# Reversed rows of W by DMA, natural channel order, unread matmuls, and split LN sums in a spectral layer with an MLP

## The chip, the cores and the metric

The kernel runs on one core of one Trainium2 chip. A core has five engines with a queue each: TensorE (PE; its weight loads are listed apart as PEld), VectorE (DVE), ScalarE (ACT), GpSimd (POOL) and SyncE (SP), which here only issues DMAs. The metric is device time in microseconds (us). Before the change three runs took 202.03, 202.07 and 204.34 us; the median is 202.07.

## The reference

Two layers on x of 2048 rows by 512 channels, bf16 in and out:

```
h   = x + spectral(layernorm(x))          # layernorm without gain, eps 1e-5
h2  = h + mlp(layernorm(h))
spectral(u) = irfft2(rfft2(u, axes rows and channels) * (w_r + 1j*w_i))   # w: 2048 x 257
mlp(v)      = relu(v @ w1 + b1)**2 @ w2 + b2                              # w1: 512 x 1792
```

## The kernel before

Rows and channels are transformed by matmuls with tables of sines and cosines that the kernel makes at the start: POOL writes index patterns, DVE or POOL multiplies them, ACT takes the sine. Row index = 16 p + g: partition p of 128, row tile g of 16, so x lies in SBUF as xs[p, g, channel].

*First stage.* For each g the kernel takes LN statistics (`ln1_stats`, lines 182–188: two DVE steps, then POOL's inverse deviation by a power), normalizes (`ln1_norm`, 190–200: DVE, or ACT for the five g in `ON_ACT`), multiplies by the tables KF on PE (`stage1`, 202–212) and ACT casts the PSUM result into Bt. It goes in chunks of x of 2, 2, 4, 4, 4 tiles, which arrive in five DMAs.

*Spectral stage.* Row frequencies k and 16 − k are handled together: pairs pr = 0 to 7 (pair 0 holds frequencies 0 and 8). `stage2` (318–327) transforms channels (table GF), ACT casts into U; `stage3` (329–352) transforms rows (table EF), ACT casts into AB; `spectral` (354–385) on DVE forms sums and differences X (the butterfly), multiplies by W (mA, mB), combines them into Z and then M; POOL does channels 0 and 256, which are real (`real_channels`); `stage4` (387–408) goes back along rows (table EI) and ACT casts into T2. Even and odd channels lie apart (e j order), in X, W and M.

*W.* Wn holds W as loaded, 16 rows a partition. POOL scales the rows 0 to 8 into WB (`w_direct`, 216–225). The rows 9 to 15 are needed with the partitions reversed: `w_reversed` (276–293) multiplies by the mirror matrix J on PE, and DVE and ACT scale the result into WB. `w_real` (295–303) makes the coefficients SD of the two real channels.

*MLP stage.* For each row tile g, `s5` (450–461) goes back along channels (table GI; DVE makes R from two halves), `s6` (463–469) finishes the rows, adds x and takes LN statistics; `rstd` (471–475) on POOL makes the inverse deviation and hb = h + b2; `norm` (480–491), `transp` (493–508). Then `up` (537–544: four matmuls, Relu on ACT, square on DVE) over 14 blocks of 128 hidden channels and `down` (548–558). Chunks are of 2, 2, 4, 4, 4 tiles (`CHUNKS`), and `run` (567–578) puts the preparation of the next chunk, step by step, between the MLP's slots of this one, in equal numbers to a slot.

Each engine takes its instructions in the order of the program: `pin` (22–31) fixes that order. Tiles of PSUM come from a pool of four buffers (first two stages) and of 3 + 3 + 2 banks (MLP stage). All loads and stores are issued on SP, in the order x, W, w1, w2, b1, b2 (lines 97–105).

Of the kernel before, what the change touches and what calls it, by code (L numbers as in the profile page):

```python
# [9 lines left out]
ALU = mybir.AluOpType  # L10
# [5 lines left out]
P = 128  # L16
# [18 lines left out]
def kernel(  # L35
# [28 lines left out]
    wrv = A_w_r.rearrange("(k j) l -> k j l", j=16)  # L64
    wiv = A_w_i.rearrange("(k j) l -> k j l", j=16)
# [9 lines left out]
    mhalf = persist.tile([P, 4], FP32, name="mhalf")  # L75
    KI = persist.tile([P, P], BF16, name="KI")
    GI = persist.tile([P, 4, 256], BF16, name="GI")
    T2 = persist.tile([P, 4, G, 16, 8], BF16, name="T2")
# [3 lines left out]
    J = fwd.tile([P, P], BF16, name="J")  # L82
    vs = fwd.tile([P, 2, 7, 2], FP32, name="vs")
    WB = [fwd.tile([P, 8, 2, 256], BF16, name=f"WB{i}") for i in range(2)]
# [15 lines left out]
    for i, wv in enumerate((wrv, wiv)):  # L100
        nc.sync.dma_start(Wn[i][:], wv)
# [12 lines left out]
    def sin_of(dst, fi):  # L114
# [18 lines left out]

    nc.gpsimd.iota(pI[:, 0:1], pattern=[[0, 1]], base=0, channel_multiplier=1)
# [5 lines left out]
    nc.gpsimd.iota(subc[:], pattern=[[0, 16], [1, 8]], base=0, channel_multiplier=0)  # L140
    nc.gpsimd.iota(idxL[:].rearrange("p (r e j) -> p r e j", r=2, e=2), pattern=[[0, 2], [1, 2], [2, 128]], base=0,
                   channel_multiplier=0)
    nc.gpsimd.memset(idxL[:, 256:257], 256)
    nc.gpsimd.memset(mhalf[:], -0.5)
    nc.gpsimd.iota(idxK[:].rearrange("p (a b) -> p a b", a=9), pattern=[[1, 9], [16, P]], base=0, channel_multiplier=0)
# [4 lines left out]
    nc.vector.scalar_tensor_tensor(fiK[:], rowA[:].rearrange("p q s -> p (q s)"), pF[:, 1:2],  # L150
                                   offA[:].rearrange("p q s -> p (q s)"), ALU.mult, ALU.add)

    nc.vector.tensor_scalar(cols[:, 0:1], pF[:, 0:1], 128.0, None, ALU.mult)
    nc.vector.tensor_scalar(cols[:, 1:2], pF[:, 0:1], 128.0, 16384.0, ALU.mult, ALU.add)

# [5 lines left out]
    nc.vector.tensor_scalar(mask[:], subc[:].rearrange("p q s -> p (q s)"), pF[:, 2:3], None, ALU.is_equal)  # L161
    for t in range(2):
        o = 512 * t
        nc.vector.tensor_scalar(fiG[:, o:o + 257], idxL[:, 0:257], cols[:, t:t + 1], float(QT), ALU.mult, ALU.add)
        nc.vector.tensor_scalar(fiG[:, o + 257:o + 512], idxL[:, 257:512], cols[:, t:t + 1], float(HT),
                                ALU.mult, ALU.add)
# [454 lines left out]
```

## Time and profile before

| | |
|---|---|
| median of the runs | 202.07 us |
| the profiled execution | 202.05 us, its span 200.3 us |
| mean granted TensorE clock | 0.939 |
| busy share PE / weight loads / DVE / ACT / POOL | 79 / 44 / 70 / 49 / 28% |
| chain that ended last, shares | PE 58%, DVE 30%, ACT 6%, POOL 3% |
| DMA | 10.27 MB in 7613 packets |

A row of a view of groups gives line, engine, operation, written tile <- read tiles, shape and count, then busy us and mean ns of one, then the idle time just before and what ended it. A row of the order of time begins with start and length in us; in brackets stands how long the engine had been idle and who released it. A row of stretches has the stretch, its length, then busy us and count of PE, weight loads, DVE, ACT and POOL, the granted clock, the DMA share and GB/s. Instructions on one engine overlap at their ends, so the distance of two starts is less than a length.

### The profile page before, as it was taken

To read this page: it belongs to the slowest core of one execution; us is meant where nothing else is said; L and a number is where in the kernel's file an instruction comes from. 1 tells how busy PE (TensorE), PEld (TensorE's weight loads), DVE (VectorE), ACT (ScalarE), POOL (GpSimd) and SP (SyncE) were. 2 spreads that over 40 slices of the span, in tenths; PEclk is the share of its full clock that TensorE was granted. 3 is DMA by queue.
4 is the path that set the end of the run, shared out by engine and by line. 5 is a ranking of instruction groups with operands and counts; after the bars stand their busy time and mean duration, and the time that the engine had idled before them with its cause. 6 is when DMAs were issued, how large, how long until landed. Compare 5 with 4: busy or idle time off the path is not lost.

```text
span 200.3 us, 2641 instructions
## 1 busy us (share of the span) xinstructions
PE 157.7 (79%) x919; PEld 88.8 (44%) x919; DVE 140.2 (70%) x320; ACT 98.5 (49%) x144; POOL 56.2 (28%) x113
## 2 busy tenths in 40 slices
PE   0046959499774450999997699999999999999992
PEld 0024846266452220774773245444554445544440
DVE  7999834958999476498699847886668878344221
ACT  3634788458886111574572357731367703488000
POOL 8558571332252006006000900008200038000000
PEclk9999999958999655699999999999999999999999
DMA  5999910000000000000100000001000000100001
GB/s 167 362 414 391 241 26 3 2 0 0 3 0 2 0 0 0 0 3 2 52 0 3 26 26 0 0 3 52 26 26 3 3 23 29 52 0 3 26 26 52
DMA packets 7613, 10.27 MB, mean 51 GB/s; under 512 B 2224, under 2 KB 6192, under 8 KB 7344
## 3 DMA queue, kind: packets, MB, share of 16 engines
q1 hardware_dynamic: 7600, 10.11, 14.8%
q8 instruction: 7, 0.11, 0.2%
q14 instruction: 6, 0.05, 0.1%
HBM read 8.01 MB, written 2.10 MB: 50 GB/s over the span
## 4 chain that ended last, share of the span: by engine, by line
PE 58%; DVE 30%; ACT 6%; POOL 3%; issue 2%; DVEq 0%; POOLq 0%; ACTq 0%
PE ph L540 22%; PE po L553 22%; DVE st L185 4%; PE p L455 4%; DVE st L468 2%; DVE mA L369 2%; ACT Bt L212 2%; DVE u L490 2%; DVE mB L369 2%; DVE hs L466 2%; PE p L502 2%; PE p L324 1%; DVE Z L371 1%; PE p L209 1%; DVE act L544 1%
## 5 line engine op out<-in xcount | busy, mean ns | idle before, releaser
L540 PE MATMUL ph<-UT,W 128*128 128x512 bf16 (+1 forms) x280 | 54.5, 341 | 0.9 <-DVE UT L508 0.5
L543 ACT ACTIVATE rl<-ph,b1f 128x512 bf16<-128x512 f32 (+1 forms) x70 | 41.5, 602 | 23.0 <-PE ph L540 20.1
L553 PE MATMUL po<-W,act 128*128 128x512 bf16 x224 | 50.8, 379 | 0.4 <-DVE act L544 0.4
L540 PEld LDWEIGHTS <-W 128*128 128x128 bf16 x280 | 27.8, 99 | 23.0 <-issue 2.7
L544 DVE TENSOR_TENSOR act<-rl 128x512 bf16<-128x512 bf16 (+1 forms) x70 | 24.8, 365 | 16.6 <-ACT rl L543 15.8
L553 PEld LDWEIGHTS <-act 128*128 128x128 bf16 x224 | 21.5, 98 | 25.0 <-DVE act L544 0.9
L472 POOL TENSOR_SCALAR rs<-mv 128x4 f32<-128x4 f32 (+1 forms) x5 | 1.3, 260 | 77.9 <-DVE mv L469 77.9
L209 PE MATMUL p<-KF,un 128*128 128x256 bf16 x32 | 10.3, 343 | 15.8 <-DVE un L199 14.7
L557 DVE TENSOR_TENSOR ot<-po,hb 128x512 bf16<-128x512 f32 x16 | 11.0, 689 | 15.1 <-PE po L553 15.1
L487 ACT ACTIVATE u<-hs,nm,rs 128x512 bf16<-128x512 bf16 x8 | 6.2, 808 | 27.3 <-DVE nm L484 27.3
L475 POOL TENSOR_TENSOR hb<-hs,b2b 128x512 f32<-128x512 bf16 x16 | 18.2, 1167 | 0.0
L400 PE MATMUL p<-EI,M 128*128 128x256 bf16 x28 | 8.2, 314 | 6.1 <-DVE M L382 6.1
L502 PE MATMUL p<-ident,u 128*128 128x128 bf16 x64 | 5.7, 231 | 8.0 <-DVE u L490 8.0
L455 PE MATMUL p<-GI,T 128*128 128x256 bf16 x64 | 10.7, 299 | 1.4 <-DVE T L406 1.4
L209 PEld LDWEIGHTS <-un 128*128 128x128 bf16 x32 | 3.8, 119 | 17.9 <-DVE un L199 15.6
L212 ACT CAST Bt<-p 128x1024 bf16<-128x1024 f32 x8 | 7.9, 1014 | 7.8 <-PE p L210 7.8
L468 DVE BATCH_NORM_STATS2 st<-hs 128x6 f32<-128x512 bf16 x16 | 11.1, 695 | 0.6
L466 DVE TENSOR_TENSOR hs<-p,xs 128x512 bf16<-128x512 f32 x16 | 10.9, 681 | 0.0
L408 ACT CAST T<-p 128x1024 bf16<-128x1024 f32 x7 | 7.1, 1014 | 7.6 <-PE p L401 3.9
L185 DVE BATCH_NORM_STATS2 st<-xs 128x6 f32<-128x512 bf16 x16 | 10.7, 668 | 0.0
L210 PE MATMUL p<-KF,un 128*128 128x256 bf16 x32 | 10.4, 346 | 0.0
L490 DVE TENSOR_SCALAR u<-hs,mv,rs 128x512 bf16<-128x512 bf16 x8 | 10.1, 1289 | 0.0
(137 smaller groups left out, 234.0 us busy)
## 6 DMA issues: line engine op xcount, KB each, us to landing
W<-in_B_w_dram SPq DMA_DIRECT2D x2, 1792.0 KB, 18.2
out_dram<-ot SPq DMA_DIRECT2D x16, 128.0 KB, 1.8
xs<-in_A_x_dram SPq DMA_DIRECT2D x3, 512.0 KB, 6.2
Wn<-in_A_w_r_dram SPq DMA_DIRECT2D x1, 1028.0 KB, 10.0
Wn<-in_A_w_i_dram SPq DMA_DIRECT2D x1, 1028.0 KB, 12.0
xs<-in_A_x_dram SPq DMA_DIRECT2D x2, 256.0 KB, 3.8
b2b<-in_B_b_dram SPq DMA_DIRECT2D x1, 128.0 KB, 8.4
b1b<-in_B_b_dram SPq DMA_DIRECT2D x1, 3.5 KB, 21.0
```

The costliest lines, as they stand in the source:

```text
L185: nc.vector.bn_stats(st[:], xs[:, g, :])
L209: nc.tensor.matmul(o, lhsT=un[:, g, P * t:P * t + P], rhs=KFlo, start=True, stop=False)
L212: nc.scalar.copy(dst, pt[:].rearrange("p (e i q s) -> p e i q s", e=4, i=2, q=16))
L455: nc.tensor.matmul(pe[:, 256 * e:256 * e + 256], lhsT=T2[:, lt, g].rearrange("p q s -> p (q s)"), rhs=GI[:, lt, :], start=(r == 0), stop=( ...
L466: nc.vector.tensor_tensor(hs[:, g, :], py[:], xs[:, g, :], ALU.add)
L468: nc.vector.bn_stats(st[:], hs[:, g, :])
L475: nc.gpsimd.tensor_tensor(hb[:, g, :], hs[:, g, :], b2b[:], ALU.add)
L490: nc.vector.tensor_scalar(u2[:, g - a, :], hs[:, g, :], mv2[:, g, 0:1], rs2[:, g:g + 1], ALU.subtract, ALU.mult)
L540: nc.tensor.matmul(ph[:, 0:n], lhsT=W1[:, d, bass.ts(f, P)], rhs=UT[:, d, 0:n], start=(d == 0), stop=(d == ND - 1))
L543: nc.scalar.activation(rl[:, 0:n], ph[:, 0:n], ACT.Relu, bias=b1f[:, f:f + 1], scale=1.0)
L544: nc.vector.tensor_tensor(act[:, f, 0:n], rl[:, 0:n], rl[:, 0:n], ALU.mult)
L553: nc.tensor.matmul(po[:], lhsT=act[:, f, bass.ts(i, P)], rhs=W2[:, f, :], start=(f == 0), stop=(f == NF - 1))
```

## The change

1. *W.* Wn, J, `w_direct` and `w_reversed` go. Two DMAs copy the rows 9 to 15 with partitions reversed from W to a scratch tile in DRAM; four load the rows 0 to 8 straight into WB; two load the scratch into WB (they wait for the copies). All stand on SP between x and w1. WB has rows of 258, of which 257 are used, unscaled: the factor WSC goes into the step of s6 that adds x.
2. *Channel order.* X, W and M are in natural order; stage 2 writes PSUM with a step of two, and stage 4 takes its weights with a step of two. T2 has the row tile outermost; its last evacuation is split 2 tiles on ACT, 7 on DVE, 7 on ACT.
3. *Unread matmuls.* `warm` issues matmuls of a tile of ones (128 x 512) whose result nobody reads: 12, 4, 4, 3 and 2 before stages 1 of g = 0, 2, 4, 8, 12, and 3, 2, 2 and 11 during the preparation of the first MLP chunk.
4. *LN sums split.* For g = 3, 7, 11, 15 ACT makes both sums (two passes that accumulate; their written result is overwritten) and POOL the variance; all normalizations are on DVE. GF's indices move from DVE to POOL, and the order of the table work changes.
5. *Order in the spectral stage.* Stage 3 and stage 2 stand ahead of stage 4 and one pair further on; the two butterfly steps of the next pair stand between those of this one; POOL's products ahead of its sums.
6. *MLP stage.* Chunks of 2, 3, 4, 4, 3; preparation steps in a new order, weighted by time and ready 2.5 (units of the weights) before the end; hb is added on POOL in `up`, each add held back until a given square; the first normalization is on DVE alone.

```diff
-    Wn = [fwd.tile([P, 16, Df], BF16, name=f"Wn{i}") for i in range(2)]
-    WB = [fwd.tile([P, 8, 2, 256], BF16, name=f"WB{i}") for i in range(2)]
+    WB = [fwd.tile([P, 8, 2, 258], BF16, name=f"WB{i}") for i in range(2)]
+    Wrev = [dram.tile([7, P, Df], BF16, name=f"Wrev{i}") for i in range(2)]
...
-        nc.sync.dma_start(Wn[i][:], wv)
+    for i in range(2):
+        nc.sync.dma_start(Wrev[i][:], wvs[i].rearrange("k j l -> j k l")[9:16, ::-1, :])
+    for i in range(2):
+        nc.sync.dma_start(WB[i][:, 0:8, 0, 0:Df], wvs[i][:, 0:8, :])
+        nc.sync.dma_start(WB[i][:, 0, 1, 0:Df], wvs[i][:, 8, :])
+    for i in range(2):
+        nc.sync.dma_start(WB[i][:, 1:8, 1, 0:Df], Wrev[i][:].rearrange("j p l -> p j l")[:, ::-1, :])
...
+    def ln1_sums(g):
+        nc.scalar.activation(un[:, g, :], xs[:, g, :], ACT.Copy, scale=1.0 / D, accum_out=mv1[:, g, 0:1])
+        nc.scalar.activation(un[:, g, :], xs[:, g, :], ACT.Square, scale=float(D) ** -0.5, accum_out=mv1[:, g, 1:2])
...
+    def ln1_rstd(a, b):
+        for g in range(a, b):
+            if g in ON_ACT:
+                nc.gpsimd.tensor_tensor(nm1[:, g:g + 1], mv1[:, g, 0:1], mv1[:, g, 0:1], ALU.mult)
+                nc.gpsimd.tensor_tensor(mv1[:, g, 1:2], mv1[:, g, 1:2], nm1[:, g:g + 1], ALU.subtract)
...
+    def warm(o, n):
+        for _ in range(n):
+            nc.tensor.matmul(o, lhsT=ones[:, 0:P], rhs=ones[:], start=True, stop=True)
...
+    ln1_rstd(0, 2)
+    ln1_sums(3)
+    sin_of(GF[:].rearrange("p t c -> p (t c)"), fiG[:])
+    ln1_stats(2, 4)
+    ln1_rstd(2, 4)
+    table_e(0)
+    ln1_sums(7)
+    ln1_norm(0, 2)
+    stage1(0, 12)
+    ln1_stats(4, 8)
+    ln1_sums(11)
+    table_e(1)
+    ln1_rstd(4, 8)
...
+    ln1_sums(15)
...
     def stage2(pr):
         pu = mm_tile("p2")
-        puv = pu[:].rearrange("p (q r e j) -> p q r e j", q=2, r=2, e=2)
+        puv = pu[:].rearrange("p (q r j e) -> p q r e j", q=2, r=2, e=2)
...
     def stage4(pr, split=False):
-                nc.tensor.matmul(o, lhsT=M[:, 0, r, c0:c0 + P], rhs=ei[:, P:3 * P], start=True, stop=False)
+                nc.tensor.matmul(o, lhsT=M[:, 0, r, e::2], rhs=ei[:, P:3 * P], start=True, stop=False)
...
         if split:
-            nc.scalar.copy(dst[:, :, :, 0:8], src[:, :, :, 0:8])
-            nc.vector.tensor_copy(dst[:, :, :, 8:16], src[:, :, :, 8:16])
+            nc.scalar.copy(dst[:, 0:2], src[:, 0:2])
+            nc.vector.tensor_copy(dst[:, 2:9], src[:, 2:9])
+            nc.scalar.copy(dst[:, 9:16], src[:, 9:16])
...
     stage2(0)
     stage2(1)
     stage3(0)
-    w_reversed()
-    w_real()
     stage3(1)
     stage2(2)
-    spectral(0)
-    for pr in range(1, 9):
-        stage4(pr - 1, split=(pr == 8))
-        if pr + 1 < 8:
-            stage3(pr + 1)
-        if pr + 2 < 8:
-            stage2(pr + 2)
+    w_real()
+    stage3(2)
+    for pr in range(9):
+        if 0 < pr and pr + 2 < 8:
+            stage3(pr + 2)
+        if pr + 3 < 8:
+            stage2(pr + 3)
+        if pr > 0:
+            stage4(pr - 1, split=(pr == 8))
         if pr < 8:
             spectral(pr)
...
-        nc.vector.tensor_tensor(hs[:, g, :], py[:], xs[:, g, :], ALU.add)
+        nc.vector.scalar_tensor_tensor(hs[:, g, :], py[:], WSC, xs[:, g, :], ALU.mult, ALU.add)
...
-    CHUNKS = ((0, 2), (2, 4), (4, 8), (8, 12), (12, 16))
+    CHUNKS = ((0, 2), (2, 5), (5, 9), (9, 13), (13, 16))
...
-            nc.vector.tensor_tensor(act[:, f, 0:n], rl[:, 0:n], rl[:, 0:n], ALU.mult)
+            sq = nc.vector.tensor_tensor(act[:, f, 0:n], rl[:, 0:n], rl[:, 0:n], ALU.mult)
+            if f % 3 == 1 and f // 3 < b - a:
+                g = a + f // 3
+                add = nc.gpsimd.tensor_tensor(hb[:, g, :], hs[:, g, :], b2b[:], ALU.add)
+                tc.add_manual_dep(add.ins, sq.ins.name,
+                                  mybir.DependencyInfo(mybir.DependencyClass.Sync, mybir.DependencyReason.DATA),
+                                  reason="not before this square")
...
+            want = len(prep) if k == len(slots) - 1 else min(len(prep), int(len(prep) * at / (total - 2.5)))
...
-    norm(0, True)
+    norm(0, False)
+    warm(idle[:], 11)
     transp(0, 0)
```

In `spectral` after the change, in the order of DVE: mA, mB, first butterfly step of the next pair, Z (two steps), second butterfly step of the next pair, M (two steps).

More of the change, by code (lines that the diff above doesn't have):

```diff
@@ L132 @@
     kft = tab.tile([P, P], BF16, name="kft")
+    nc.vector.memset(ones[:], 1.0)
     nc.gpsimd.iota(pI[:, 0:1], pattern=[[0, 1]], base=0, channel_multiplier=1)
@@ L166 @@
                                 ALU.mult, ALU.add)
-    sin_of(kft[:], fiK[:])
-    sin_of(GF[:].rearrange("p t c -> p (t c)"), fiG[:])
-    nc.vector.tensor_tensor(KF[:, 0:P], kft[:], mask[:], ALU.mult)
-    nc.vector.tensor_scalar(KF[:, P:2 * P], KF[:, 0:P], -1.0, None, ALU.mult)
-    for i, off in ((0, 0), (1, QT)):
-        nc.gpsimd.tensor_scalar(fiE[i][:], idxK[:], cols[:, 3:4], float(off), ALU.mult, ALU.add)
-        nc.scalar.activation(
-            EF[:, :, i, :], fiE[i][:].bitcast(I16)[:, ::2].rearrange("p (a b) -> p a b", a=9), ACT.Sin,
-            scale=SIN_SCALE)
+    nc.gpsimd.iota(idxK[:].rearrange("p (a b) -> p a b", a=9), pattern=[[1, 9], [16, P]], base=0, channel_multiplier=0)
```

257 lines of the change are left out of this document (119 added, 138 removed).

## The prediction

> **What bounds the kernel now.** I read the page's clock line first, then busy time by stretches cut at the stage borders, then the order of time on each engine inside the stretches that lose. The time outside the span is 202.05 − 200.3 = 1.75 us; the profiled execution (202.05) is at the median of the runs (202.07), so I sum against it.
>
> The page's span and the granted clock in 40 slices of 5 us, then stretches (length; busy us of PE, weight loads, DVE, ACT, POOL; granted clock):
>
> ```profile
> span 200.3 us, 2641 instructions
> PEclk9999999958999655699999999999999999999999
> 40.00:46.00 6.00, 5.87 (x27) 3.72 (x28) 3.64 (x9) 3.04 (x3) 1.88 (x8) 0.50 0.00 0
> 51.80:55.50 3.70, 2.94 (x21) 1.84 (x20) 3.50 (x9) 2.94 (x4) 1.04 (x5) 1.00 0.02 4
> 66.75:81.00 14.25, 5.87 (x27) 3.15 (x27) 7.73 (x15) 2.73 (x5) 3.45 (x6) 0.50 0.00 0
> 80.96:96.73 15.77, 15.64 (x104) 10.35 (x104) 11.21 (x29) 8.30 (x18) 3.39 (x4) 0.92 0.03 10
> 96.70:117.45 20.75, 16.80 (x123) 10.99 (x121) 17.87 (x41) 10.23 (x21) 5.80 (x6) 1.00 0.04 13
> 117.45:145.00 27.55, 27.55 (x148) 13.78 (x148) 19.84 (x42) 13.20 (x21) 5.78 (x6) 1.00 0.06 20
> 173.00:196.80 23.80, 23.71 (x110) 10.54 (x108) 8.29 (x18) 9.62 (x14) 0.00 (x0) 1.00 0.07 23
> ```
>
> From 117.45 on PE is busy the whole time at full clock: 27.55 us for four row tiles with the preparation of four others, 23.80 for four without. So a row tile's MLP costs 5.95 us, a preparation 27.55/4 − 5.95 = 0.94, and sixteen and fourteen of them 95.2 + 13.2 = 108.4 us. Before does it from 80.96 to 196.8, 115.8 us: only 7.4 us can be won there. Of these 96.70–117.45 loses most: two tiles and four preparations are 15.7 us of PE work in 20.75, with DVE busy 17.87. The rest must come from the first 81 us, of which 20.25 us run at half clock.
>
> **First stage, to the first spectral matmul.** DVE sets it; groups by line (count, busy, mean ns), the first statistics, the first stage 2 matmul:
>
> ```profile
> L185 DVE BATCH_NORM_STATS2 st<-xs 128x6 f32<-128x512 bf16 x16 | 10.7, 668 | 0.0
> L186 DVE BATCH_NORM_AGGREGATE mv<-st 128x2 f32<-128x6 f32 x16 | 2.9, 182 | 0.6
> L199 DVE TENSOR_SCALAR un<-xs,mv,rs 128x512 bf16<-128x512 bf16 x11 | 4.1, 422 | 0.0
> L164 DVE TENSOR_SCALAR fiG<-idxL,cols 128x257 int32<-128x257 int32 x2 | 2.4, 1208 | 0.0
> L196 ACT ACTIVATE un<-xs,nm,rs 128x512 bf16<-128x512 bf16 x5 | 4.0, 814 | 0.9 <-DVE nm L193 0.9
> L173 ACT ACTIVATE EF<-fiE 128x1152 bf16<-128x1152 int16 x2 | 2.2, 1146 | 0.0
> L116 ACT ACT_TABLE_LOAD x1 | 1.3, 1283 | 0.7 <-PEq L605 0.7
> L188 POOL TENSOR_TENSOR rs<-rs,mhalf 128x4 f32<-128x4 f32 (+1 forms) x5 | 4.6, 919 | 0.4
> L172 POOL TENSOR_SCALAR fiE<-idxK,cols 128x1152 int32<-128x1152 int32 x2 | 2.7, 1352 | 0.2
> 0.72 2.28 SPq L99 DMA_DIRECT2D xs<-in_A_x_dram  x5
> 6.91 0.69 DVE L185 BATCH_NORM_STATS2 st<-xs 128x6 f32<-128x512 bf16 x1
> 27.30 1.93 ACT L212 CAST Bt<-p 128x1024 bf16<-128x1024 f32 x2
> 29.29 1.92 PE L324 MATMUL p<-GF,Bt 128*128 128x256 bf16 x16 [1.15 <-ACT Bt L212]
> DMA to landing us min/median/max: 3.0/5.4/7.9
> ```
>
> The change takes from DVE four pairs of statistics (4 × 0.85 = 3.4) and the G table's indices (two of 1.21 and two short ones, about 2.8 in sequence); five normalizations come back (5 × 0.42 = 2.1), a fill of ones is new (about 0.2, like other small ones). DVE is relieved by 3.9 us and begins LN at 6.91 − 2.8 + 0.2 = 4.3; it may, because the first chunk of x, issued at 0.72, lands after 3.0 us, at 3.7, and the last, issued by 2.6 (the five issues take 2.28 us), after 7.9, at 10.5. POOL takes the indices where it otherwise waits.
>
> ACT gets eight passes of about 0.81 instead of five, and there they stand in a chain. The second chunk lands at about 5.7 (its landing is the next above 3.0); the sums of tile 3 are done at 7.4, then POOL makes the inverse deviation (0.92 for the power and about 0.7 for the three short steps before it, an estimate from the 0.18 and 0.2 of small ones) and the table's indices (1.35), so the sine starts at 10.4. From there ACT's queue is sine 1.15, sums of tile 7 1.5, cast 0.95, sums of 11 1.5, sine 1.15, cast 0.95, sums of 15 1.5, then six casts at a pitch of 0.93 (two back to back took 1.93): 10.4 + 8.7 + 5.6 = 24.7. What an accumulating pass costs beyond 0.81 no row shows; between nothing and 0.4 each, I take 0.15 for each of eight: 26.0. Gain **3.3 us** (29.3 − 26.0), between 1.3 and 3.9. The fillers before stage 1 need only the ones and run while PE waits for DVE's normalizations; the twelve first take about 5 us at half clock and are through before DVE's first tile. Not costed; without that cover a group of four would hold up its stage 1 by 0.9. The negated table moves on DVE and costs the same. POOL's pass over W goes; nobody waited for it.
>
> **Spectral stage.** The evacuation that gives the first X, the first multiplication with W, DVE's one long wait, one steady period, the last M:
>
> ```profile
> 32.52 1.01 ACT L343 CAST X<-p 128x1024 bf16<-128x1024 f32 x1 [0.23 <-PE pwx L279]
> 35.34 0.68 DVE L369 TENSOR_TENSOR mA<-X,WB 128x1024 bf16<-128x1024 bf16 x1
> 43.86 0.45 DVE L362 TENSOR_TENSOR X<-AB 128x512 bf16<-128x512 bf16 x1 [2.23 <-ACT AB L352]
> 52.15 0.42 DVE L363 TENSOR_TENSOR X<-AB 128x512 bf16<-128x512 bf16 x1
> 52.60 0.72 DVE L369 TENSOR_TENSOR mA<-X,WB 128x1024 bf16<-128x1024 bf16 x1
> 53.24 0.68 DVE L369 TENSOR_TENSOR mB<-X,WB 128x1024 bf16<-128x1024 bf16 x1
> 53.95 0.42 DVE L371 TENSOR_TENSOR Z<-mA,mB 128x512 bf16<-128x512 bf16 x1
> 54.85 0.42 DVE L382 TENSOR_TENSOR M<-Z 128x512 bf16<-128x512 bf16 x1
> 55.52 0.42 DVE L362 TENSOR_TENSOR X<-AB 128x512 bf16<-128x512 bf16 x1
> 66.33 0.42 DVE L384 TENSOR_TENSOR M<-Z 128x512 bf16<-128x512 bf16 x1
> ```
>
> Three things go. (1) The reversal by matmul with its two evacuations stands between X (33.5) and the product (35.34): 1.8 us. (2) The 2.23 us wait: stage 3 of pair 2 was queued on PE behind a stage 4 that waited for POOL, then ran at the 0.50 clock of 40–46. The new order puts stages 3 and 2 ahead of stage 4 and one pair earlier, so ACT has each AB about 1 us before DVE wants it; in a full period (51.80–55.50) PE and ACT are busy 2.9 us each, so neither reaches DVE's new period. (3) In the period of 3.71 us (52.15 to 55.52, and the 0.34 of the first butterfly, now of the next pair) every step that needs its predecessor starts late: mA 0.45 after the butterfly instead of 0.34, Z 0.71 after mB instead of 0.61, M 0.90 after the first Z instead of 0.68, while M's two steps and the butterfly follow at 0.34 each (54.85 to 55.52). The interleaved butterflies fill these: 6 × 0.34 + 2 × 0.61 = 3.27 us, a saving of 0.44 × 7 = 3.1, next late is then DVE's own work. With 0.8 for pair 0, whose butterfly wait and product waits go too, 1.8 + 2.2 + 3.1 + 0.8 = **7.9 us**; from the first stage 2 to the last M 37.5 becomes 29.6. Strided weights and the strided PSUM output have no row in this trace; PE has 0.3 us a pair to spare, so from 0 to 2 us lost; I take 0, nearest to the loads of this window, which run beside the matmuls (1.84 us in 2.94). The scale of W moves into an add that reads the same elements; taken as nothing.
>
> **The W loads** decide whether that holds. The queue from 20 to 24 us, when rows of 1 KB and of 2 bytes mix (packets, MB, share of 16 engines), and the output rows (last number: us to landing):
>
> ```profile
> q1 hardware_dynamic: 2577, 1.18, 112.5%
> out_dram<-ot SPq DMA_DIRECT2D x16, 128.0 KB, 1.8
> ```
>
> 2577 packets took 1.125 × 16 × 4 = 72 engine-us, 28 ns each at a mean of 458 bytes. A row of 257 bf16 is 514 bytes: about 30 ns. Reversed copy, direct load and reversed load are 1792, 2304 and 1792 rows: over sixteen engines 3.4, 4.3 and 3.4 us behind x (10.5), with 1.8 us for each landing, so about 23.4. The sync queue waits for the copy, and W1, W2 and the biases wait behind it (3.7 MB, 12 us more at this window's 1.18 MB in 4 us, wanted after 45 us): that costs nothing. The reversed rows are wanted by POOL's sums at S + 4 (S = 26.0, the first spectral matmul), by DVE at S + 7: 30 to 33 us. POOL waits there, and behind it stand the real channels of pair 0, stage 4 of pair 0 on PE and ACT's cast of it. No transfer from DRAM to DRAM stands in the trace, so its row price is 28 ns from below and twice that from above, 60, for reading and writing DRAM. I take a stall of **2 us**, between 0 and 13 (seven engines at 60 ns, worked out below).
>
> **Hand-over and MLP.** First stage 5 matmul, then the end of the first LN2:
>
> ```profile
> 69.88 1.86 PE L455 MATMUL p<-GI,T 128*128 128x256 bf16 x8 [1.40 <-DVE T L406]
> 77.22 2.26 POOL L475 TENSOR_TENSOR hb<-hs,b2b 128x512 f32<-128x512 bf16 x2
> 77.28 1.10 DVE L484 SCALAR_TENSOR_TENSOR nm<-mv,rs 128x2 f32<-128x2 f32 x1 [1.27 <-POOL rs L473]
> 78.30 1.32 DVE L490 TENSOR_SCALAR u<-hs,mv,rs 128x512 bf16<-128x512 bf16 x1
> 80.96 1.01 PE L540 MATMUL ph<-UT,W 128*128 128x256 bf16 x4 [0.25 <-ACT UT L506]
> ```
>
> From the last M (66.75) to the first MLP matmul are 14.2 us. The negated mean and one normalization ran 1.10 and 1.32 us, ending as the two adds for hb on POOL end; with the adds moved and both normalizations on DVE (0.42 each as L199) that is 0.8 instead of 2.4: −1.6. The split copy lets stage 5 begin after two of 16 tiles, without most of the 1.40 us wait for DVE's half; but three fillers of 512 columns stand before it on PE. At half clock eight matmuls of 256 columns took 1.86 with the last one's way out, 0.21 each, so the fillers take 1.3 and give this back. The second part of DVE's chain gets about 0.3 longer, its order now waiting once for stage 6. Gain **1.8 us**, between 0.8 and 3. The eleven fillers before the transposes run inside a wait of about 3.5 us for DVE and POOL; if they raise the clock, 80.96–96.73 (clock 0.92) gains 15.77 × 0.08 = 1.3.
>
> MLP: chunk 0 now prepares three tiles instead of two and chunk 1, with three, four. Before, DVE was busy 11.2 us with two preparations beside two tiles and 17.87 with four: 3.3 for each. So chunk 0 asks 14.5 of DVE, and 2 × 5.95 + 3 × 0.94 = 14.7 of PE. In the 14.5 about 2 are steps that stood beside hb's adds, as 1.10 and 1.32 above; without them 12.5. But the moved adds, three in this chunk at 1.13, now stand beside squares, and if each holds one as long, DVE has 12.5 + 3.4 = 15.9, more than PE. Chunk 1 has 21.6 on PE and by the same count about 20.7 on DVE. I leave 3.2 us of loss there, the middle between the 1.2 that this leaves in chunk 0 and the 5.1 that 96.70–117.45 lost: 108.4 + 3.2 = 111.6 against 115.8, **4.2 us** with the clock's 1.3. The Trainium skill, "SBUF — State Buffer", section "Who interferes with whom", says that the pair of ports which VectorE and GpSimd share is held exclusively for a whole instruction, and that a VectorE step with two SBUF inputs is blocked by a GpSimd step that reads SBUF. The trace agrees at 1.10 us for a step on two numbers per partition; by the rule the 15.9 holds and chunk 0 loses 1.2 at least; if only steps like 77.28 and 78.30 waited, the 12.5 would, and the sum would come out 1.2 lower.
>
> **Sum**: 3.3 + 7.9 − 2 + 1.8 + 4.2 = 15.2; 202.05 − 15.2 = **187 us**. With every term at its good end (0.6 and 1.2 more from the first stage and the hand-over, no stall, 2 less MLP loss) 181; with the first stage, strided weights, hand-over and MLP at their bad ends (2 + 2 + 1 + 1.9) 194, before any stall beyond 2.
>
> **Rivals.** (A) *The reversed rows come too late*, the slower side. Their copy has an outer dimension of 7. If it runs on seven engines, each has 256 rows of it, 144 direct rows queued behind, 112 reversed ones: 512 × d after 10.5, + 1.8. At 30 ns that is 27.7 and costs nothing; from 34 ns on DVE waits; at 60 ns 43.0, a stall of 13 and 198; from 76 ns on 51.2, a stall of 21, 206 and slower than before. For it: nothing in the trace shows such a copy, and everything later waits. Against: 28 ns in the measured mix, and 1.8 us for a whole output tile of 1 KB rows to DRAM. Seven engines are an even chance by the rows, 60 ns or more with them 0.3: 0.16, of which 0.07 beyond 206.1. The Trainium skill, "DMA: Bandwidth & Descriptors", section "Why a DMA increments its semaphore by 16 and not by 1", says that a transfer runs on the largest number of engines up to 16 that divides the slowest dimension of both sides, here 7. No row of this trace shows another case than 128; by the page 27.7 would hold in place of 23.4, both without a stall at 30 ns.
>
> (B) *ACT becomes the bound of the first stage*: if Square wants another function table than Sin, each change costs another load of 1.28 us (one in the rows above), seven of them 9 us on the chain that ends at 26.0: 196. Against: Identity, Copy, Relu and Sin share one load. 0.07. (C) *The clock stays low and the adds collide*: the fillers hold up stage 5, 0.50 lasts into the MLP, chunk 0 loses as much as chunk 1 did: 1 + 1.3 + 1.9 more, 191. 0.15. The forecast itself: 0.62.
>
> Measurement tells about 2% (198.0 and 206.1) from no change. Faster is the forecast, B and C: 0.84; within 2% the middle of A: 0.09; slower 0.07. The range is 181 to 197: below it 0.06, above it A, 0.13 or so.
>
> **What would show it.** Right: the first spectral matmul near 26 us; no wait over 0.5 us on DVE from there to the last M, its period 3.3; reversed W landed before 30; clock 1.0 at the first MLP matmul; normalizations at 0.4. Wrong: DVE or POOL waiting for a W transfer; a second function table load; accumulating passes far over 0.8; PE waiting for weights in stage 4; a stretch in chunk 0 or 1 where PE waits for squares.

## The result, and the profile after

The changed kernel takes 194.5 us (median; 193.75 to 197.05) against 203.2 for the kernel before on the same chip: a ratio of 0.956, with a 95% interval of 0.946 to 0.966. The ratio leaves out the one slow execution, that of 197.05 us. The forecast was 187, so the direction was right and a little under half of the gain is missing. The profiled execution took 193.75 us, 8.3 less than the 202.05 of the prediction.

The page of the changed kernel, its span and the granted clock in 40 slices of 4.8 us:

```profile
span 192.0 us, 2699 instructions
PEclk9979999999999699999999999999999999999999
```

The same kernel by stretches, cut at the borders that the prediction used: first spectral matmul (24.68), last M (60.56), first MLP matmul (73.98), then the first two chunks (columns as before: length; busy us of PE, weight loads, DVE, ACT, POOL; granted clock; DMA share; GB/s):

```profile
0.00:24.68 24.68, 17.49 (x109) 10.36 (x109) 21.06 (x59) 17.58 (x29) 18.66 (x49) 0.93 0.79 201
24.68:60.56 35.88, 29.33 (x165) 17.61 (x165) 26.15 (x63) 23.55 (x24) 14.03 (x41) 1.00 0.36 112
60.56:73.98 13.42, 8.89 (x44) 4.39 (x44) 6.12 (x15) 2.13 (x5) 1.23 (x4) 0.87 0.00 0
73.98:91.40 17.42, 15.62 (x112) 10.32 (x112) 11.95 (x35) 8.96 (x19) 3.42 (x4) 1.00 0.03 9
91.40:115.30 23.90, 22.70 (x136) 12.29 (x134) 17.13 (x41) 11.72 (x21) 4.74 (x5) 1.00 0.05 17
```

Stage by stage, before, forecast and after:

| stretch | before | forecast | after |
|---|---|---|---|
| to the first spectral matmul | 29.3 | 26.0 | 24.7 |
| to the last M | 37.5 | 29.6 (+2 stall) | 35.9 |
| to the first MLP matmul | 14.2 | 12.4 | 13.4 |
| to the last MLP matmul | 115.8 | 111.6 | 114.5 |

The first stage gained more than forecast. The spectral stage, which was to give most, gave 1.6 us. Its granted clock is 1.00 throughout, so the clock does not explain it. TensorE is busy 29.33 of 35.88 us there. The groups of TensorE by line show where (count, busy us, mean ns); first the changed kernel, stage 2 and the second half of stage 4:

```profile
L315 PE MATMUL p<-GF,Bt 128*128 128x256 bf16 x64 | 15.0, 417 | 1.0 <-ACT Bt L222 1.0
L400 PE MATMUL p<-EI,M 128*128 128x256 bf16 x28 | 6.6, 274 | 0.2
```

and the kernel before: the same stage 2 over the whole span, then stage 2 and stage 4 from 46.8 to 63 us alone, where its granted clock is full:

```profile
L324 PE MATMUL p<-GF,Bt 128*128 128x256 bf16 x64 | 9.0, 291 | 1.1 <-ACT Bt L212 1.1
...
L324 PE MATMUL p<-GF,Bt 128*128 128x256 bf16 x32 | 4.1, 272 | 0.0
L401 PE MATMUL p<-EI,M 128*128 128x256 bf16 x16 | 3.7, 275 | 0.2
```

Stage 2 has the same 64 matmuls of the same shape and operands. It now writes its PSUM columns with a step of two, and one takes 417 ns in place of 291, or of 272 where the clock was full as it is now. Stage 4 reads its weights with a step of two and takes 274 ns against 275. The order of time shows what follows from it. One loop of the changed kernel (start, duration, engine, line; in brackets the idle time before and what ended it):

```profile
43.91 1.01 ACT L318 CAST U<-p 128x1024 bf16<-128x1024 f32 x1 [0.64 <-PE p L315]
...
44.97 0.38 PE L338 MATMUL p<-U,EF 128*128 128x512 bf16 x1 [0.28 <-ACT U L318]
...
45.83 1.89 PE L315 MATMUL p<-GF,Bt 128*128 128x256 bf16 x8
46.06 0.69 DVE L361 TENSOR_TENSOR mB<-X,WB 128x1024 bf16<-128x1024 bf16 x1
...
46.16 1.01 ACT L343 CAST AB<-p 128x1024 bf16<-128x1024 f32 x1 [0.33 <-PE p L341]
...
47.21 0.43 DVE L352 TENSOR_TENSOR X<-AB 128x512 bf16<-128x512 bf16 x1 [0.46 <-ACT AB L343]
...
47.81 1.01 ACT L318 CAST U<-p 128x1024 bf16<-128x1024 f32 x1 [0.64 <-PE p L315]
```

Cast of U, stage 3, stage 2, and again the cast of U: 43.91 to 47.81, 3.90 us. Stage 3 waits for the cast, stage 2 stands behind stage 3 in TensorE's queue, the next cast waits for stage 2. AB hangs on this loop, and DVE waits for it in six of the seven pairs that have one, 3.8 us in all, here 0.46. The eight matmuls of stage 2 hold TensorE 1.7 us (from 45.83 to 47.52, when stage 4 begins), 0.21 us each; in the plain form below eight take 1.04 us with the way out of the last, 0.11 each.

### The profile page after: what moved, and what is told of

Read it like the earlier page. It is cut to its first block, busy times and chain, and to the rows that moved or that the text cites. A ratio compares the mean times of both kernels' runs of the same rounds, so it can differ in the third digit from the quotient of the medians.

```text
span 192.0 us, 2699 instructions
## 1 busy us (share of the span) xinstructions
PE 166.8 (87%) x946; PEld 91.3 (48%) x946; DVE 129.1 (67%) x308; ACT 97.3 (51%) x152; POOL 57.1 (30%) x117
## 4 chain that ended last, share of the span: by engine, by line
PE 59%; DVE 23%; ACT 9%; POOL 5%; issue 2%; ACTq 0%; POOLq 0%; DVEq 0%
PE ph L544 19%; PE po L563 19%; PE p L315 7%; DVE act L548 4%; ACT U L318 4%; DVE st L474 3%; DVE hs L470 3%; DVE st L195 3%; PE p L455 3%; DVE un L208 2%; PE p L506 2%; DVE R L464 2%; DVE R L465 2%; POOL rs L479 1%; ACT u L491 1%
## 5 line engine op out<-in xcount | busy, mean ns | idle before, releaser
L547 ACT ACTIVATE rl<-ph,b1f 128x384 bf16<-128x384 f32 (+2 forms) x70 | 41.9, 602 | 23.7 <-PE ph L544 22.0
L544 PE MATMUL ph<-UT,W 128*128 128x384 bf16 (+2 forms) x280 | 52.9, 336 | 0.5 <-ACT UT L510 0.5
L548 DVE TENSOR_TENSOR act<-rl 128x384 bf16<-128x384 bf16 (+2 forms) x70 | 32.3, 478 | 13.0 <-ACT rl L547 12.7
L563 PEld LDWEIGHTS <-act 128*128 128x128 bf16 x224 | 21.6, 98 | 26.9 <-issue 2.7
L315 PE MATMUL p<-GF,Bt 128*128 128x256 bf16 x64 | 15.0, 417 | 1.0 <-ACT Bt L222 1.0
L219 PE MATMUL p<-KF,un 128*128 128x256 bf16 x32 | 8.0, 290 | 4.8 <-DVE un L208 4.8
L318 ACT CAST U<-p 128x1024 bf16<-128x1024 f32 x8 | 8.1, 1012 | 6.9 <-PE p L315 6.9
L315 PEld LDWEIGHTS <-Bt 128*128 128x128 bf16 x64 | 8.2, 130 | 6.4 <-ACT Bt L222 1.1
L470 DVE SCALAR_TENSOR_TENSOR hs<-p,xs 128x512 bf16<-128x512 f32 x16 | 10.8, 678 | 0.6 <-PE p L469 0.5
L227 PE MATMUL p<-ones 128*128 128x512 bf16 x25 | 8.7, 497 | 1.4 <-DVE ones L139 1.4
L469 PE MATMUL p<-R,KI 128*128 128x512 bf16 x16 | 6.1, 380 | 3.4 <-DVE R L465 3.2
```

The source lines that it names most:

```text
L227: nc.tensor.matmul(o, lhsT=ones[:, 0:P], rhs=ones[:], start=True, stop=True)
L315: nc.tensor.matmul(puv[:, q, :, e, :], lhsT=Bt[:, 2 * t + e, 2 * pr + q, :], rhs=GFv[:, t, :, e, :], start=(t == 0), stop=(t == 1))
L318: nc.scalar.copy(U[:].rearrange("p q c -> p (q c)"), pu[:])
L470: nc.vector.scalar_tensor_tensor(hs[:, g, :], py[:], WSC, xs[:, g, :], ALU.mult, ALU.add)
L544: nc.tensor.matmul(ph[:, 0:n], lhsT=W1[:, d, bass.ts(f, P)], rhs=UT[:, d, 0:n], start=(d == 0), stop=(d == ND - 1))
L547: nc.scalar.activation(rl[:, 0:n], ph[:, 0:n], ACT.Relu, bias=b1f[:, f:f + 1], scale=1.0)
```

## The experiments

All were timed in three rounds beside the kernel before; the time of the changed kernel itself is the 0.956 above. The kernel before took 203.3 us there, but 201.7 on the chip of combo2 and combo3, so across chips the ratios are to be compared. Where stages are compared, the numbers are those of one profiled execution each.

**Stage 2 with contiguous PSUM columns (s2_plain).** The natural order is kept, but ScalarE's cast restores it:

```diff
-        puv = pu[:].rearrange("p (q r j e) -> p q r e j", q=2, r=2, e=2)
+        puv = pu[:].rearrange("p (q r e j) -> p q r e j", q=2, r=2, e=2)
...
-        nc.scalar.copy(U[:].rearrange("p q c -> p (q c)"), pu[:])
+        nc.scalar.copy(U[:].rearrange("p q (r j e) -> p (q r) j e", r=2, e=2),
+                       pu[:].rearrange("p (x e j) -> p x j e", x=4, e=2))
```

> Stage 2 writes its PSUM columns next to each other again (in the order its weights' companions GF deliver them), and ScalarE's cast of U puts them into natural order, reading PSUM with a step; all else as in the changed kernel. Theory: the step of two in stage 2's PSUM output halves TensorE's rate there (417 ns mean against 291) and that alone keeps the loop U cast, stage 3, AB cast, DVE late. Then the mean of the stage 2 group falls back to 290 to 310 ns, the first two stages 2 take about 1.9 us in place of 3.64, the period of the pairs falls from 3.9 to 3.3 to 3.5 us, DVE no longer waits over 0.5 us for AB, and the time falls from 194.5 to about 188.5 us (187.5 to 190). Rival: the cost belongs to the natural order itself and only changes its engine, the U cast with a stepped read rising from 1.02 us to 1.5 to 2: then DVE still waits for AB, the period stays at 3.7 to 4.0 us and the time is 192 us or more.

Measured: 189.4 us, ratio 0.926 (0.918 to 0.935). The cast of U stays at 1.02 us with its stepped read. The groups of this kernel's TensorE:

```profile
L315 PE MATMUL p<-GF,Bt 128*128 128x256 bf16 x64 | 8.1, 273 | 1.0 <-ACT Bt L222 1.0
```

and its stretch from the first spectral matmul to the last M:

```profile
24.66:54.93 30.27, 21.35 (x159) 15.10 (x163) 25.25 (x63) 21.65 (x23) 18.22 (x42) 0.99 0.49 151
```

The stretch falls from 35.88 to 30.27 us, by 5.6. DVE's waits for AB are gone, and the period is 3.22 us (mA at 32.02, 35.23, 38.45, 41.66 in the chain of waits), DVE's own work. The theory holds and the rival falls: the step cost TensorE, and costs ScalarE nothing here.

With that out of the way a new wait shows, in the order of time of the same kernel:

```profile
48.60 3.97 POOL L431 CAST b1f<-b1b 128x14 f32<-128x14 bf16 x1
48.62 0.68 DVE L362 TENSOR_TENSOR mB<-X,WB 128x1024 bf16<-128x1024 bf16 x1
...
51.84 0.68 DVE L362 TENSOR_TENSOR mB<-X,WB 128x1024 bf16<-128x1024 bf16 x1
52.54 0.20 POOL L297 TENSOR_TENSOR ta<-SD,AB 128x4 f32<-128x4 f32 x1
...
53.46 0.28 PE L400 MATMUL p<-EI,M 128*128 128x256 bf16 x1 [4.71 <-POOL M L303]
```

A cast of 14 numbers per partition, 0.19 us in the changed kernel, takes 3.97 beside a DVE that now works without a gap, and TensorE idles 4.7 us behind GpSimd's real channels.

**The cast of b1 moved behind the loop (s2_b1f)**, on top of s2_plain:

```diff
-            nc.gpsimd.tensor_copy(b1f[:], b1b[:])
+    nc.gpsimd.tensor_copy(b1f[:], b1b[:])
```

> As the kernel with the plain stage 2, and the cast of b1 on GpSimd (3.97 us there, at 48.60, while DVE ran without a gap) goes behind the spectral loop. Theory: DVE's uninterrupted run of bf16 steps keeps GpSimd's cast from ending, GpSimd's products of pairs 5 to 7 come late, TensorE idles 4.7 us for them and its clock is halved at the end of the stage. With the cast moved, GpSimd's small sums find no such long wait (none over 1.5 us), TensorE's wait of 4.7 us is gone or split into pieces under 2 us, the last M comes at about 54.0 us in place of 54.9, the first MLP matmul at 66.5 to 67.8 in place of 68.8, and the time falls by 1 to 2.5 us against the plain stage 2 (189.4 median, 188.6 in its profile), to 186.5 to 188. Rival: any instruction of GpSimd is held in the same way, so the first products take the cast's place: then the waits stay and the time falls by less than 0.5 us.

Measured: 188.5 us, ratio 0.929 (0.920 to 0.938), no difference from s2_plain that these intervals allow. The cast takes 0.20 us in its new place, GpSimd's products of the next pair 0.74 in the old one, and the wait of 4.7 us is two of 1.3 and 1.4. So the rival is wrong about the wait, and the theory about the time: the last M came only 0.6 us earlier (54.35), and half of that was lost again by the first MLP matmul (68.52 against 68.80 us), because TensorE's clock was low for longer. Stretches of this kernel (the number ahead of the DMA share is the granted clock):

```profile
52.00:54.00 2.00, 0.61 (x4) 0.21 (x3) 1.83 (x6) 1.11 (x2) 0.86 (x3) 1.00 0.00 0
54.00:56.00 2.00, 1.92 (x8) 1.15 (x9) 0.36 (x2) 0.00 (x0) 0.59 (x3) 0.50 0.00 0
58.00:60.00 2.00, 2.00 (x9) 1.06 (x8) 0.00 (x0) 0.00 (x0) 0.00 (x0) 0.50 0.00 0
```

Half clock from 54 to over 60 us, on the chain of the hand-over; in s2_plain the clock is full again by 58. Why the cast is held and the products beside it are not, no run shows.

**No b2 additions (no_hb).**

```diff
-            if f % 3 == 1 and f // 3 < b - a:
+            if False:
...
-                nc.vector.tensor_tensor(ot[:], po[:], hb[:, g, :], ALU.add)
+                nc.vector.tensor_tensor(ot[:], po[:], hs[:, g, :], ALU.add)
```

> The additions of b2 to hs on GpSimd (hb) are left out, and the output adds hs alone, so b2 is missing from the result; nothing else is changed. Theory: each of them holds the squares that fall beside it to its own length (squares of 1.00 to 1.04 us against 0.3), and TensorE waits for those in the short chunks. Then the squares' group mean falls from 478 ns to under 345, the first two chunks (73.98 to 115.3, 41.3 us) take 38.5 to 39.5, and the time falls by 2 to 2.5 us to about 192. Rival: the first two chunks wait for their preparation's chain, not for squares: then the squares shorten as much, but the chunks stay above 40.8 us and the time falls by 0.5 us or less.

Measured: 193.4 us, ratio 0.951 (0.946 to 0.956). In the changed kernel's order of time, first, a pair of squares without an addition and the next one beside an addition:

```profile
75.12 0.73 DVE L548 TENSOR_TENSOR act<-rl 128x256 bf16<-128x256 bf16 x2 [1.13 <-ACT rl L547]
...
75.93 1.15 POOL L551 TENSOR_TENSOR hb<-hs,b2b 128x512 f32<-128x512 bf16 x1 [3.79 <-DVE act L548]
76.44 1.00 DVE L548 TENSOR_TENSOR act<-rl 128x256 bf16<-128x256 bf16 x2 [0.58 <-ACT rl L547]
```

The groups of DVE without the additions:

```profile
L548 DVE TENSOR_TENSOR act<-rl 128x384 bf16<-128x384 bf16 (+2 forms) x70 | 25.5, 366 | 18.4 <-ACT rl L547 17.8
```

The squares' mean falls from 478 ns to 366, not below 345, but the first two chunks fall only from 41.15 us to 40.2 and the whole MLP stage from 114.5 to 113.2: between theory and rival. The additions do hold the squares; by chunk that is worth 0.3 us (17.27 to 17.00), 0.6, nothing, 0.4 and nothing. In this execution the hand-over was 1.2 us longer, at a mean clock of 0.68 against 0.87, with the same program, so the time shows less than the MLP stage gained.

**No fillers (no_fill).** No matmul that nobody reads is issued (`for _ in range(n)` becomes `range(0)`).

> All filler matmuls (those nobody reads) are left out: 25 in the first stage and 18 in the hand-over. Theory: they are worth a little on both sides. Without them the first three of the hand-over (1.4 us at half clock, ahead of stage 5) are gone and the hand-over's stage 5 starts about 1 us earlier, but the granted clock reaches full only after the first MLP matmul, which costs 1 to 2 us in chunk 0; the first stage changes by 0 to 1 us. The time stays within 193.5 to 196. Rival A: the fillers hold the clock up where it matters: first stage and first chunk each lose 2 us or more and the time is 198 or more. Rival B: they only stand in the way: 193 or less.

Measured: 195.0 us, ratio 0.957 (0.953 to 0.961). The first spectral matmul comes at 24.2 us (0.5 earlier), the hand-over takes 12.5 us (0.9 less), the first chunk 19.3 (2.0 more; its clock is 0.50 until about 76). The theory holds: what the fillers cost ahead, the clock returns behind, and as placed they are worth nothing that can be told.

**LN statistics back on DVE (ln_back)**: the four token groups' sums on ScalarE and their variances on GpSimd left out, statistics of all sixteen on DVE, five normalizations on ScalarE, as in the kernel before.

```diff
-            if g not in ON_ACT:
+            if True:
                 st = fwd.tile([P, 6], FP32, tag="st", bufs=4, name="st")
...
+            if g in (3, 7, 11, 13, 15):
+                nc.scalar.activation(un[:, g, :], xs[:, g, :], ACT.Identity, bias=nm1[:, g:g + 1],
+                                     scale=rs1[:, g:g + 1])
```

> The first LayerNorm goes back to the split of the kernel before: all statistics on DVE, normalizations of g = 3, 7, 11, 13 and 15 on ScalarE, no sums by accumulating passes; all else as in the changed kernel. Theory: the DVE work that ScalarE's passes took over (4 statistics against 5 normalizations taken back) is what shortened the first stage together with the freer ScalarE, so the first spectral matmul moves from 24.7 us to 26 to 28, and the time rises by 1.5 to 3.3 us to 196 to 198. Rival: the first stage is shorter because the work on rows 1 to 7 of W and its wait are out of it and the loads of x come first, whatever the split: the first spectral matmul stays below 25.5 and the time changes by under 0.8 us.

Measured: 198.6 us, ratio 0.972 (0.966 to 0.978), a little beyond the theory's 196 to 198. The first spectral matmul comes at 26.5 us, 1.8 later. Another 3 us of its profile lie where the granted clock is 0.50, from 62 to 70 us and from 78 to 80: the hand-over takes 14.5 us in place of 13.4, the first chunk 19.3 in place of 17.3. So of the first stage's 4.6 us the split gives 1.8, and 2.8 come from the rest (the table's indices off DVE, the work on W out of the stage); no run tells these apart.

**The chunks of before (old_chunks).**

```diff
-    CHUNKS = ((0, 2), (2, 5), (5, 9), (9, 13), (13, 16))
+    CHUNKS = ((0, 2), (2, 4), (4, 8), (8, 12), (12, 16))
```

> The changed kernel with the chunks of the kernel before (2, 2, 4, 4, 4 token groups in place of 2, 3, 4, 4, 3). Theory: the new sizes shorten the MLP stage, since the second chunk's matmuls cover more of the third's preparation: with the old ones the stretch from the first MLP matmul to the last grows from 114.5 us to 115.3 to 116.5, and the time by 0.8 to 2 us, to 195.3 to 196.5. Rival: the chunks trade a stall at chunk 1 for one at chunk 2 and are worth nothing: the stretch stays at 114.5 plus or minus 0.5 and the time at 194.5 plus or minus 0.7.

Measured: 197.2 us, ratio 0.970 (0.962 to 0.978); the stretch of the MLP is 117.9 us, more than either theory said. The second chunk now takes 20.84 us for 15.7 us of TensorE's work, against 23.88 for 21.6: 2.9 us of stall gone by the new sizes. Some of the time is the clock's, which this edit did not touch. It is 0.70, 0.50 and 0.95 in the three stretches of 2 us from 74 to 80, which loses about 1.7 us, an estimate from these shares; without it the stretch would be about 116.2, inside the theory's range. The hand-over is 0.7 us longer, also at half clock.

**No copy through scratch (no_wrev).** The rows 9 to 15 are not reversed.

```diff
-        nc.sync.dma_start(Wrev[i][:], wvs[i].rearrange("k j l -> j k l")[9:16, ::-1, :])
+        pass
...
-        nc.sync.dma_start(WB[i][:, 1:8, 1, 0:Df], Wrev[i][:].rearrange("j p l -> p j l")[:, ::-1, :])
+        nc.sync.dma_start(WB[i][:, 1:8, 1, 0:Df], wvs[i][:, 9:16, :])
```

> The copy of the reversed rows of W through DRAM scratch is left out: the rows 9 to 15 of each k are loaded straight and unreversed, so that the filter is wrong for them; all else as in the changed kernel. Theory: the copy was done in time and its traffic lay beside DVE's work, so without it b1, the first spectral matmul (24.7 us) and the last M (60.6) move by less than 0.5 us, and the time stays at 194.5 plus or minus 0.7. Rival: the copy's packets hold back the loads of x or of W, and its wait GpSimd's preparation of the filter: then the first spectral matmul comes 0.8 us or more earlier, and the time falls below 193.7.

Measured: 193.9 us, ratio 0.954 (0.949 to 0.960); first spectral matmul at 24.8 us, last M at 60.7. The theory holds: the route costs nothing that can be told.

**A better version.** Three kernels build on s2_b1f. The first, combo:

```diff
-            nc.scalar.copy(dst[:, 0:2], src[:, 0:2])
-            nc.vector.tensor_copy(dst[:, 2:9], src[:, 2:9])
-            nc.scalar.copy(dst[:, 9:16], src[:, 9:16])
+            nc.scalar.copy(dst[:, :, 0:2], src[:, :, 0:2])
+            nc.vector.tensor_copy(dst[:, :, 2:4], src[:, :, 2:4])
...
-            if f % 3 == 1 and f // 3 < b - a:
-                g = a + f // 3
+            for g in range(a, b) if f == NF - 1 else ():
...
-    warm(idle[:], 3)
     s5(0)
```

> Meant as a better version: the plain stage 2 and the moved cast of b1; the last evacuation of the spectral stage split by PSUM bank (ScalarE half, DVE half, at the same time) and not by tokens in three; the first three fillers of the hand-over left out; the b2 additions of a chunk all issued after its last square, so that they lie beside its second matmul. Theory: against the kernel with the first two of these, the hand-over loses 0.8 us of serial evacuation and 0.7 to 1.3 us of fillers, and the squares' mean falls from 479 ns to under 390, which gives 1 to 1.7 us in the first two chunks: 184 to 185.5 us in all. Rival: the hand-over's gain is paid back by a clock that is halved at the first MLP matmul, and the additions then hold up DVE's preparation of the next chunk: 186.5 us or more.

Measured: 186.9 us, ratio 0.917 (0.910 to 0.925). The two halves of the evacuation still ran one after the other (55.38 and 56.00 us). The squares' mean is 366 ns. The first MLP matmul comes at 66.7 us, 1.8 earlier than in s2_b1f, in part because stage 4 of the last pair ran at full clock (its last matmul starts at 55.07 against 55.67); but the MLP stage is 1.0 us longer, for the clock is halved again at its start, as the rival said. The theory's 184 to 185.5 us did not come.

The second, combo2, has one cast in place of the split (`split=False`).

> As the kernel called combo, and the last evacuation of the spectral stage not split at all: one cast on ScalarE, like those of the other pairs. Theory: the parts of the split ran one after the other (1.32 us in combo, 1.49 with three parts), since the program orders all writes to that tile; one cast takes 1.02. So the time between the last stage 4 matmul and the first stage 5 matmul falls by 0.3 us, and the time from 186.9 to about 186.5 us, the clock's dips staying (halved for 3 us in the hand-over and again at the first MLP matmuls). Rival: the split's parts overlap in part or the cast alone is longer here: no change or up to 0.5 us slower.

Measured: 187.1 us, ratio 0.925 (0.916 to 0.934): the first stage 5 matmul comes 0.34 us earlier (56.40 against 56.74), as worked out. The profiled executions differ by as much (187.07 against 187.44 us); the medians and ratios are too wide to show it. The third, combo3, adds fillers where TensorE idled ahead of a halving:

```diff
         pt = mm_tile("p4")
+        warm(pt[:, 0:512], {6: 5, 7: 6}.get(pr, 0))
...
+    warm(idle[:], 3)
     s5(0)
...
-    warm(idle[:], 11)
+    warm(idle[:], 16)
```

> As combo2, with fillers where TensorE was seen to idle over 1 us ahead of each halving of the clock: five before stage 4 of pair 6, six before that of pair 7, the three before stage 5 kept, sixteen in place of eleven before the first transposes. Theory: each idle stretch of 1.3 to 1.4 us is followed about 3 us later by some 3 us at half clock (combo: idle to 54.07, half from about 57 to 60; idle to 65.36, half from 67.5 to 70.5), and covered waits keep the clock at 1.00 from 46 to 80 us. That returns 1.4 us in the hand-over's chain and 1.5 in the first MLP matmuls: about 184 us, 2 to 3 less than combo2. Rival: the clock falls by the sum of work over a longer time or by something no filler changes, and the fillers only stand in the way: 186.5 or more.

Measured: 185.2 us, ratio 0.915 (0.909 to 0.921), four executions between 185.15 and 185.20. Stretches of combo2, with the granted clock ahead of the last two numbers:

```profile
52.00:54.00 2.00, 0.55 (x4) 0.21 (x3) 1.83 (x5) 1.06 (x2) 0.80 (x3) 1.00 0.00 0
58.00:60.00 2.00, 2.00 (x7) 0.60 (x4) 1.15 (x3) 0.37 (x1) 0.00 (x0) 0.52 0.00 0
64.00:66.00 2.00, 0.79 (x8) 0.54 (x9) 0.83 (x3) 0.32 (x1) 0.48 (x1) 1.00 0.00 0
68.00:70.00 2.00, 2.00 (x12) 1.36 (x10) 0.29 (x1) 1.14 (x3) 0.00 (x0) 0.50 0.00 0
```

and of combo3:

```profile
52.00:54.00 2.00, 2.00 (x14) 1.17 (x13) 1.83 (x5) 1.01 (x1) 0.72 (x2) 1.00 0.00 0
58.00:60.00 2.00, 1.24 (x6) 0.29 (x3) 1.41 (x4) 0.41 (x2) 0.00 (x0) 1.00 0.00 0
64.00:66.00 2.00, 1.40 (x11) 0.64 (x10) 1.03 (x3) 0.52 (x1) 0.28 (x1) 1.00 0.00 0
68.00:70.00 2.00, 1.78 (x17) 1.35 (x14) 1.28 (x5) 1.87 (x6) 0.00 (x0) 1.00 0.00 0
```

Where TensorE has little to do (0.55 and 0.79 of 2 us), half clock follows within 4 us in combo2; with the gaps filled it does not come. All four executions of combo3 have a mean clock of 1.0, and none of the 40 of the changed kernel and its nine other variants has. So fillers can keep the clock up, and the rival falls. The theory that each such gap brings half clock is too strong, though. The wait before the first transposes is 1.26 us in s2_b1f as in combo2, and there the clock stays full behind it, as it does in s2_plain and in the changed kernel:

```profile
66.00:68.00 2.00, 0.72 (x8) 0.54 (x9) 0.74 (x2) 0.12 (x1) 0.68 (x1) 1.00 0.00 0
68.00:70.00 2.00, 1.55 (x16) 1.33 (x14) 0.70 (x2) 1.25 (x3) 0.00 (x0) 1.00 0.00 0
70.00:72.00 2.00, 2.00 (x20) 1.70 (x18) 1.33 (x5) 1.94 (x6) 1.15 (x1) 1.00 0.03 8
```

What decides between the two, no run shows. The time is 1.9 us less by the medians, a little under the 2 to 3 expected. In the hand-over the three fillers put stage 5 off by 0.57 us (56.97 against 56.40), and the full clock returns little more than that: the first MLP matmul is only 0.2 us earlier (66.12 against 66.32). The rest comes from the first chunk (17.67 against 19.34 us).

## Why the prediction was right or wrong

**First stage (forecast 3.3, measured 4.6).** The direction was right, the chain was not, and 4.6 lies above the range's good end of 3.9. I let ScalarE's queue end the stage; in the trace ScalarE waits 1.05 us for TensorE before its last two casts, and the chain of waits runs through DVE's statistics and normalizations. An accumulating pass costs less than the 0.96 us I took. Two rows of the changed kernel's ScalarE:

```profile
5.07 0.63 ACT L188 ACTIVATE un<-xs 128x512 bf16<-128x512 bf16 x1 [2.55 <-DMA xs<-in_A_x_dram]
5.60 0.18 ACT L188 ACTIVATION_READ_ACCUMULATOR un<-xs 128x1 f32 x1
```

The next pass starts at 5.82, so a pass with its read-out is 0.75. Copy and Square share Sin's table: one load, as before. ScalarE as the bound (rival B) is out. That my sum for ScalarE without a margin, 24.7, equals the measured start is chance, for another chain set it.

**Spectral stage (forecast 37.5 to 29.6, measured 35.9).** The step that failed is "Strided weights and the strided PSUM output have no row in this trace ... I take 0, nearest to the loads". It cost 5.6 us (35.88 against 30.27), and I allowed 2. Weights and output were put into one term with one bound. They behave differently: the weights' step of two costs nothing (274 ns), the output's doubles the pitch, from 0.11 to 0.21 us. My bound "from 0 to 2 us" came from TensorE's spare time of 0.3 us a pair; it did not ask what happens if stage 2 becomes part of a loop with ScalarE's cast. The 16 matmuls at the start took 3.63 us (24.68 to 28.31; before 1.92), and with 0.85 us more in each later pair (1.89 against 1.04) that loop became 3.90 us against DVE's 3.22. The other steps of this term were right, as s2_plain shows: 30.27 us against 29.6, the period 3.22 against 3.27, and no DVE wait for AB.

A rule spoke against the change and I did not weigh it. The Trainium skill, "SBUF — State Buffer", section "Door 1: The DMA port swizzle", says in passing that PSUM has 8-byte cache lines, two fp32 values, and that any non-contiguous PSUM access slows matmuls significantly. The trace agrees for the output of a matmul, 417 against 273 ns. For ScalarE's stepped read of PSUM no cost is seen (1.02 us both ways).

**Reversed W (forecast −2, range 0 to −13; measured 0).** GpSimd's two rows that read it, in the changed kernel:

```profile
24.97 0.23 POOL L288 TENSOR_TENSOR SD<-WB 128x14 f32<-128x14 bf16 x1 [1.36 <-DMA WB<-Wrev]
27.23 0.22 POOL L289 TENSOR_TENSOR SD<-WB 128x14 f32<-128x14 bf16 x1 [2.04 <-DMA WB<-Wrev]
```

It has landed by 27.2 us, within the "before 30" of the prediction, and the next user waits for ScalarE's X until 30.35. So GpSimd does wait for W, which the prediction named as a sign of being wrong, but off the chain. Rival A did not come. The 27.2 is near the 27.7 that the prediction worked out for seven engines, and not the 23.4 for sixteen; and from 10 to 12 us, behind the loads of x, the packets take 54% of sixteen engines' time, where it was 90% from 5 to 9. This speaks for fewer engines and doesn't show it, for the two reversed loads were issued only at 19.4 and 19.9 us. By the prediction's own working neither number is late at 30 ns a row.

**Hand-over (forecast 1.8, measured 0.8).** The normalizations went as worked out, 0.74 us for both against 2.4 with the mean. The split is what failed, in the changed kernel's order of time:

```profile
61.59 0.27 ACT L404 CAST T<-p 128x128 bf16<-128x128 f32 x1 [1.68 <-PE p L400]
61.89 0.62 DVE L405 CAST T<-p 128x448 bf16<-128x448 f32 x1 [1.33 <-ACT T L404]
62.55 0.53 ACT L406 CAST T<-p 128x448 bf16<-128x448 f32 x1 [0.69 <-DVE T L405]
63.13 1.44 PE L227 MATMUL idle<-ones 128*128 128x512 bf16 x3 [1.58 <-ACT T L406]
```

I counted on stage 5 starting after the first part. Each part waits for the one before, the first filler waits for the last, and the three fillers at half clock (to 64.37) stand behind that: 3.8 us from the last M to stage 5, before 3.1. One undivided cast takes 1.02 us, less than the three parts' 1.49. The kernel before already had a split in two, and its trace shows the same wait, which I read over:

```profile
68.52 0.59 ACT L405 CAST T<-p 128x512 bf16<-128x512 f32 x1 [3.44 <-PE p L401]
69.14 0.69 DVE L406 CAST T<-p 128x512 bf16<-128x512 f32 x1 [2.39 <-ACT T L405]
```

**MLP (forecast 4.2, measured 1.3).** Full clock at the first MLP matmul came as forecast; without the fillers the first chunk takes 2.0 us more (no_fill). The new chunk sizes did what they were meant for in the second chunk (2.9 us, old_chunks). The loss that I left, 3.2 us, was mis-sized: 114.5 − 108.4 is 6.1. By chunk it is 2.6, 2.3, 0.1, 0.8 and 0.5.

For the first chunk I counted three additions and 15.9 us of work on DVE. There are two additions, one for each row tile of the chunk, and DVE is busy 11.95 us, under the 12.5 that I had without them. The Trainium skill, "SBUF — State Buffer", "Who interferes with whom", has the rule of an exclusive hold, and the trace agrees: a pair of squares takes 1.00 us beside an addition of 1.15, and 0.73 without one. But the "1.2 at least" in the first chunk that I worked out by it did not come: without any addition that chunk is 0.3 us shorter, and the whole stage 1.4. The other 4.7 us of the loss lie elsewhere. In the first chunk TensorE waits 1.4 us for R and 0.3 for u, two steps of the preparation, and the 108.4 took no such wait. The rest of it stays open.

**Rival C** (clock low, additions collide, 191). The additions collide, but the clock was full at the first MLP matmul, and the first chunk lost 2.6 us and not 5.1. The time of 194.5 lies beyond it for a reason none of the rivals held: the mechanism that I had priced at nothing. That 194.5 is inside the range of 181 to 197 is luck. My terms at their bad ends gave 194 with a stall of 2 us for W; that stall was 0, which leaves 192, and the room above was kept for late rows of W, which did not come late.

## What to carry to other kernels

An access pattern that the trace of before does not show should be priced apart for each operand, and against the loop that it would lengthen, not against the engine's spare time alone. Let the engine that evacuates PSUM do the reordering: here its cast cost the same with a stepped read, while a stepped matmul output doubled the pitch. Put fillers by the places where TensorE idles in the 4 us ahead of a clock drop, and off the chain; as placed in the changed kernel, three of them at the head of the chain, they gave back what they won. Look in the trace of before for whether two engines that write parts of one tile ran side by side at all.

## What the runs showed that was not expected

- A PSUM output step of two (fp32) doubles a matmul's pitch, 0.11 to 0.21 us for 256 columns at full clock; the same step in the weights costs nothing.
- A GpSimd cast of 14 numbers per partition took 3.97 us beside an uninterrupted run of two-input bf16 steps on DVE, 0.19 to 0.20 otherwise.
- Waits of 1.3 to 1.4 us in TensorE's work were in some executions followed within 4 us by 3 us or more at half clock, and in others not, the same wait in the same place. With them filled, four executions ran at full clock and agreed within 0.05 us, where the other kernels here spread over 0.4 to 3.6.
